# Attention followed by a spectral mix on one core: q and k transposed in one pass, one pair's x moved ahead of a chunk, idle products at two places

## The chip, the core and the metric

The kernel runs on one core of a Trainium2 chip. The metric is the device time of one execution in microseconds (us). The kernel before takes 443.85 us, the median of three runs (443.67 to 444.85). The profile was taken in a run of 444.44 us and spans 442.4 us; all times of single instructions below count from the start of that span.

A core has five engines with a queue each, and each works its queue strictly in order: TensorE (PE in the profile, with PEld for its weight loads), VectorE (DVE), ScalarE (ACT), GpSimd (POOL) and SyncE (SP). Transfers between memory and the core's SBUF run on 16 DMA engines; here GpSimd and SyncE issue them. TensorE writes its results to PSUM, from where VectorE or ScalarE copies them.

## What is computed

There are 8 batches of 8 heads with 576 tokens and head size 64. Causal attention with a bias from a running sum of `s` gives x with 512 features per token; then the tokens are mixed in the frequency domain with 64 complex modes, and a dense layer with relu follows.

```python
# attention, per batch and head
scores = q @ k.T / sqrt(64)
cum    = cumsum(max(s, 0))
scores = where(causal, -1e9, scores + min(-(cum[:, None] - cum[None, :]), 0))
x      = softmax(scores) @ v                     # heads side by side: 512 features
# mix of the tokens
X = rfft(x, axis=tokens)[:64 modes]
Y = complex product of X with (w_r + i w_i)      # one 512x512 matrix per mode
u = x + irfft(Y)
out = u + max(u @ w_ch, 0)
```

The weights `w_r` and `w_i` are 64 matrices of 512x512 each, in float32 in memory, and are turned into bf16 by the transfer. They are most of what the kernel reads.

## The kernel before

**Attention.** The heads go in pairs: there are N = 32 steps n, each for one batch and two heads (n = 8 g + b, with g the group of 128 features and b the batch). A step works like this. `transposes(n + 1, half)` (lines 332 to 347) turns q and k of the next step around: the loaded tile holds q on partitions 0 to 63 and k on partitions 64 to 127 (two heads of 32 rows each), and every row holds 18 tokens one after the other. For nine tokens of a half, a 64x64 product transposes q into PSUM partitions 0 to 63 and another transposes k into partitions 64 to 127, 18 small products in all. Then two copies of 64x576 take q to the tile `qt` and k to the tile `kt`: in the first half both on VectorE, in the second half q on VectorE and k on ScalarE. The PSUM tile `tr_ps` has one buffer, so the second half's products follow the first half's copies. `scores` (line 366) multiplies keys and queries and takes the exponential on ScalarE (line 390), `av` (line 401) multiplies with v and divides by the sum on VectorE (lines 423 to 428), `fft` (line 435) takes the token transform of the step before, with four copies on VectorE (line 453).

The order of the work in a step is written out by hand (lines 564 to 592): scores of the first head, `av` of the step before, mode products if there are any, `transposes(n+1, 0)`, scores of the second head, `transposes(n+1, 1)`, `fft(n-1)`, `av(n, 0)`. In the last six steps (n = 26 to 31) x of six pairs of token tiles is transposed and multiplied with `w_ch` as well, in two parts of a step (`first_transposed`, `first_product`); the second part's product follows a copy on VectorE (line 538).

**The weights.** GpSimd issues all loads of q, k, v and the weights (line 234), in the order of their use. Weights come in tiles of four modes, 256 KB per transfer and two transfers per tile; a buffer is loaded again once its last product is done. `modes(g, c)` (line 455) multiplies chunk c (eight modes) of group g: 16 products, four for each of the chunk's four weight tiles.

**The end.** After attention the chunks of the last group (g = 3) come one by one (lines 833 to 856); between them lies work that doesn't need the weights: x of the remaining pairs is transposed (`x_transposed`, line 629) and multiplied with `w_ch` (`x_times_wch`, line 641), and y of each chunk is transposed (`y_transposed`), multiplied (`y_times_wch`) and spread (`gather`, `spread`). In the kernel before, x of pair 1 is transposed after the products of chunk 6, and multiplied with `w_ch` between y of chunk 6 and its product (lines 852 to 856). The products of chunk 7, the last, come in four lots of four, numbered 0 to 3 (line 471); lots 0 and 1 use the real weights, lots 2 and 3 the imaginary ones. Ahead of lot 2 stand ten products for the results of pair 0 (`first_u`, `first_z(0)`), ahead of lot 3 eight for pair 1 (`first_z(1)`), line 868. After lot 3 the last y is finished and the 18 pairs of output tiles follow in a list written out by hand (lines 924 to 930).

PSUM tiles with the tag `aux` share two buffers in turn, at the end for the products of a chunk (`yp`), the transposed y (`yt_ps`) and its product (`v_ps`).

Of the kernel before, what the change touches and what calls it, by code (L numbers as in the profile page):

```python
# [9 lines left out]
FP32 = mybir.dt.float32  # L10
FP16 = mybir.dt.float16
BF16 = mybir.dt.bfloat16
# [6 lines left out]
def kernel(  # L19
# [11 lines left out]
    nc = tc.nc  # L31
    B, H, S, D = q.shape
    NM = moe_w_r.shape[0]
    DM = H * D
    P = 128
# [4 lines left out]
    NG = DM // P  # L40
# [6 lines left out]
    NCK = NM // MC  # L47
# [4 lines left out]
    RP = P // 4  # L52
    R = S // RP
    RH = R // 2
    W = 2 * P
    NWN = S // W
    NK = 2 * NWN
    HM = NM // 2
    HP = P // 2
# [45 lines left out]
    ident16h = gp.tile([P, P], FP16, name="ident16h")  # L105
    Ff_sb = gp.tile([P, NT, 3 * NM], FP16, name="Ff_sb")
    G_sb = gp.tile([P, SP], FP16, name="G_sb")
    wch_sb = gp.tile([P, DT, DM], FP16, name="wch_sb")
# [12 lines left out]
    NQ = 2  # L121
# [165 lines left out]
    with tc.tile_pool(name="cum_psum", bufs=1, space=PSUM) as cpsum:  # L287
        spos = s_sb
        zer, cum = (p_sb[i][:NPAIR, :].bitcast(FP32)[:, :S] for i in (0, 1))
        nc.vector.memset(zer, 0.0)  # L290
        nc.vector.tensor_scalar(out=spos, in0=s_sb, scalar1=0.0, scalar2=None, op0=ALU.max)
        nc.vector.tensor_tensor_scan(
            out=cum, data0=spos, data1=zer, initial=0.0, op0=ALU.add, op1=ALU.add
        )
        nc.vector.tensor_scalar(out=ncum_sb, in0=cum, scalar1=-8.0, scalar2=None, op0=ALU.mult)
        ct_ps = cpsum.tile([P, NK + 1, NPAIR], FP32, name="ct_ps")
        keys = cum[:, : NF * P].rearrange("c (w p r) -> c w r p", p=P, r=2)
        for x in range(NK):
            nc.tensor.transpose(
                ct_ps[:, x, :], keys[:, x // 2, x % 2, :], ident32[:NPAIR, :NPAIR]  # L300
            )

        tl = p_sb[2][:NPAIR, :].bitcast(FP32)[:, : 2 * NL].rearrange("p (x t) -> p x t", x=2)
        for x in range(2):
            nc.vector.tensor_copy(out=tl[:, x, :], in_=cum[:, (NT - 1) * P :])
        nc.tensor.transpose(
            ct_ps[:, NK, :], tl.rearrange("p x t -> p (x t)"), ident32[:NPAIR, :NPAIR]
        )
        nc.vector.tensor_copy(out=cumt_sb, in_=ct_ps)
        for x in range(2):  # L310
            rows = slice(NL * x, NL * x + NL)
            nc.vector.tensor_copy(
                out=cumt4[rows, :], in_=cumt_sb[rows, NK, x::2]
            )
# [17 lines left out]
    def transposes(n, half):  # L332
        if n >= N:
            return
        src = loaded[n][:, n % 2, :].rearrange("p (r d) -> p r d", d=D)[:, half * RH : half * RH + RH]
        ps = trpool.tile([P, RH, 2 * RP], BF16, name="tr_ps", tag="tr")
        for r in range(RH):
            for i in range(2):
                rows = slice(HP * i, HP * i + HP)
                nc.tensor.transpose(ps[rows, r, :], src[rows, r, :], ident16[rows, rows])  # L340
        for i, dst in enumerate((qt, kt)):
            copy = (nc.vector.tensor_copy, nc.scalar.copy)[half * i]
            to = dst[n % NQ][:D].rearrange("d h (p r) -> d h p r", r=R)
            copy(  # L344
                out=to[:, :, :, half * RH : half * RH + RH],
                in_=ps[HP * i : HP * i + HP].rearrange("d r (h p) -> d h p r", h=2),
            )

    def scores4(n, ps):

# [293 lines left out]
    def x_times_wch(i, last):  # L644
        for x in range(2):
            start_z(i, x)
            for dt in range(DT):
                nc.tensor.matmul(  # L648
                    zs[i, x], xts[i][:, x, dt, :], wch_sb[:, dt, :],
                    start=(dt == 0), stop=(last and dt == DT - 1), skip_group_check=True,  # L650
                )
# [25 lines left out]
    def y_times_wch(c, yt):  # L677
        vp = auxpool.tile([P, DM], FP32, name="v_ps", tag="aux")
        for dt in range(DT):
            nc.tensor.matmul(  # L680
                vp, yt[:, dt, :], wch_sb[:, dt, :], start=(dt == 0), stop=(dt == DT - 1)
            )
        vb = spool.tile([P, DM], FP16, name="v_sb", tag="v")
        nc.vector.tensor_copy(out=vb, in_=vp)
        spread(c, 1, vb)
        return vb

    def gather(c0, c1, turns, kinds):

        n = 2 * MC * (c1 - c0)  # L690
        rows = slice(2 * MC * c0, 2 * MC * c1)
        ng = P // n
        for b0 in range(0, B, ng):
            for which in kinds:
                ps = auxpool.tile([P, DM], FP32, name="g_ps", tag="aux")
                for dt in range(DT):
                    for g in range(ng):
                        op = yt_first[:, dt, : c1 - c0].rearrange("p c (x b) -> p (c x) b", b=B)
                        nc.tensor.matmul(
                            ps[n * g : n * g + n, :] if which else ps[n * g : n * g + n, bass.ts(dt, P)],  # L700
                            op[:, :, b0 + g],
                            wch_sb[:, dt, :] if which else ident16h,
                            start=(dt == 0 or not which), stop=(dt == DT - 1 or not which),
                            tile_position=(0, n * g), skip_group_check=True,
                        )
                for g in range(ng):
                    dst, src = yv[rows, b0 + g, which, :], ps[n * g : n * g + n, :]
                    if g % 2:
                        nc.vector.tensor_copy(out=dst, in_=src)
                    else:  # L710
                        nc.scalar.copy(out=dst, in_=src)
            if b0 // ng in turns:
                work()
# [119 lines left out]
    for c in range(NCK - 2):  # L833
        yb = modes(NG - 1, c)
        for x in range(TAKE[c] - 1):
            work()
        if c == NCK - 3:
            x_transposed(0)
        yt = y_transposed(yb, c)
        if TAKE[c]:  # L840
            work()
        if c >= NY:
            if c == NCK - 3:
                x_times_wch(0, False)
            y_times_wch(c, yt)
            if c == NCK - 3:
                gather(NY, NCK - 2, (), (0,))
        elif c == NY - 1:
            gather(0, NY, (1, 3), (1, 0))
    assert not order_z and not ahead  # L850
    c = NCK - 2
    yb6 = modes(NG - 1, c)
    x_transposed(1)
    yt = y_transposed(yb6)
    x_times_wch(1, False)
    vb6 = y_times_wch(c, yt)


    def first_u():
        add_x(0)  # L860
        add_y(u_of(0), 0, 0, slice(0, GK))
        add_last(u_of(0), 0, yb6, c=0)

    def first_z(i):
        add_y(z_of(i), i, 1, slice(0, GK))
        add_last(z_of(i), i, vb6, c=0)

    yb = modes(NG - 1, NCK - 1, {2: lambda: (first_u(), first_z(0)), 3: lambda: first_z(1)})

    yt = spool.tile([P, DT, P], FP16, name="yt_sb", tag="yt")  # L870
    for x in range(2):
# [95 lines left out]
```

The softmax here doesn't subtract the row's maximum and nothing guards it: scores larger than these inputs give would overflow.

## Time and profile before

| | before |
|---|---|
| median of 3 runs | 443.85 us |
| profiled span | 442.4 us |
| TensorE busy, products | 340.4 us (77%), 4364 instructions |
| VectorE busy | 253.3 us (57%) |
| ScalarE busy | 226.2 us (51%) |
| bytes moved | 93.25 MB, mean 211 GB/s |
| attention, first q and k products to the end of its last step | 10.7 to about 336 us |
| first products of the last chunk of weights | 403.5 us |
| last transfer of weights issued | 397.2 us |
| first output transfer issued | 413.4 us |

The page has one row for each group of instructions: line, engine, operation, what it writes and reads, shape and count, then busy time and mean duration of one in ns, then the idle time of the engine ahead of them and what ended it. Its second part cuts the span into 40 slices of 11.06 us and gives busy tenths; PEclk is the granted TensorE clock in tenths. The chain of waits follows the work that ended last back to the start. The timeline gives merged rows in order of time: start, length, engine, line, operation, count, and in brackets the idle time ahead.

### The profile page before, as it was taken

The numbers are of one execution on the slowest core, as the hardware profiler recorded it, in microseconds if no ns is written. First come the engines' busy times: TensorE is split into PE (matmuls) and PEld (weight loads), VectorE is DVE, ScalarE is ACT, GpSimd is POOL, SyncE is SP. The second block draws the span as 40 slices with busy tenths as digits, with TensorE's granted clock in tenths as the row PEclk, the third lists the DMA queues.
The fourth block names the chain that finished last, engine by engine and source line by source line (L and its number), as shares of the span: only waits on it lengthen the run. The fifth ranks groups of instructions, "written<-read, shape, count | busy, mean of one in ns | idle before, by whom it ended". The sixth has DMA issues, their size and how long they took to land.

```text
span 442.4 us, 10783 instructions
## 1 busy us (share of the span) xinstructions
PE 340.4 (77%) x4364; PEld 208.2 (47%) x4411; DVE 253.3 (57%) x574; ACT 226.2 (51%) x421; POOL 246.1 (56%) x385
## 2 busy tenths in 40 slices
PE   1788988988776996593946918888887987759994
PEld 0455665655444653361634505555653445423441
DVE  7766776665645664462633605767655454442696
ACT  1476787365645643472543604665660534320794
POOL 7766565565565656455655546455544444440495
PEclk9998999998969798987895978999997999988998
DMA  9999999999999999999999999999999999997498
GB/s 180 202 208 204 204 206 205 206 207 206 208 195 206 205 208 205 209 206 209 203 206 206 208 207 198 207 206 206 202 209 211 209 209 210 210 217 150 147 388 344
DMA packets 72768, 93.25 MB, mean 211 GB/s; under 512 B 29760, under 2 KB 31296, under 8 KB 72720
## 3 DMA queue, kind: packets, MB, share of 16 engines
q0 software_dynamic: 63408, 81.29, 104.9%
q1 hardware_dynamic: 9312, 11.29, 7.6%
q8 instruction: 34, 0.56, 0.5%
q14 instruction: 14, 0.11, 0.1%
HBM read 163.51 MB, written 9.44 MB: 391 GB/s over the span
## 4 chain that ended last, share of the span: by engine, by line
DMA 60%; PE 19%; DVE 7%; POOL 6%; issue 4%; ACT 2%; POOLq 0%; DVEq 0%
DMA w_sb<-in_moe_w_i_dram 31%; DMA w_sb<-in_moe_w_r_dram 16%; DMA qk<-in_k_dram 8%; PE yp L463 4%; PE sc_ps L382 3%; DMA x_all<-in_moe_w_r_dram 2%; POOL w_sb L234 2%; DMA qk<-in_q_dram 2%; PE sc_ps L376 2%; DMA y_acc<-in_moe_w_r_dram 2%; PE z_ps L546 2%; DVE xt L538 2%; DVE xs L453 1%; PE z_ps L648 1%; PE av_ps L418 1%
## 5 line engine op out<-in xcount | busy, mean ns | idle before, releaser
L390 ACT ACTIVATE p_sb<-sc_ps,cumt_sb 128x576 f16<-128x576 f32 (+1 forms) x256 | 141.7, 635 | 34.3 <-PE sc_ps L382 33.9
L234 POOL DMA_DIRECT2D w_sb<-in_moe_w_r_dram x120 | 71.2, 595 | 63.2 <-DMA w_sb<-in_moe_w_i_dram 16.7
L234 POOL DMA_DIRECT2D w_sb<-in_moe_w_i_dram x120 | 70.9, 593 | 53.0 <-DMA w_sb<-in_moe_w_i_dram 18.7
L344 DVE COPY qt<-tr_ps 64x576 bf16<-64x576 bf16 x64 | 47.8, 747 | 55.7 <-PE tr_ps L340 55.6
L234 POOL DMA_DIRECT2D v<-in_v_dram x72 | 52.0, 722 | 36.6 <-DMA w_sb<-in_moe_w_r_dram 7.6
L382 PE MATMUL sc_ps<-qt,kt 128*128 128x320 bf16 (+2 forms) x337 | 66.7, 303 | 7.2 <-ACT kt L344 3.4
L340 PE MATMUL tr_ps<-ident,qk 64*64 64x64 bf16 x1152 | 35.4, 206 | 38.9 <-DMA qk<-in_k_dram 18.0
L463 PE MATMUL yp<-w_sb,xs 128*32 128x512 bf16 (+1 forms) x480 | 43.2, 413 | 23.8 <-DMA w_sb<-in_moe_w_i_dram 16.8
L361 ACT ACTIVATE p<-sc_ps,cumt 128x64 f16<-128x64 f32 x32 | 10.0, 313 | 88.7 <-PE sc_ps L357 88.7
L376 PE MATMUL sc_ps<-negm,ident 128*128 128x256 bf16 x256 | 53.8, 295 | 0.0
L382 PEld LDWEIGHTS <-kt 128*128 128x128 bf16 x384 | 39.0, 105 | 31.1 <-ACT kt L344 8.8
L340 PEld LDWEIGHTS <-qk 64*64 64x64 bf16 x1152 | 26.9, 119 | 55.2 <-DMA qk<-in_k_dram 19.0
L418 PE MATMUL av_ps<-v,p_sb 128*128 128x65 f16 x1024 | 43.8, 197 | 1.4 <-DVE x_all L428 1.0
L418 PEld LDWEIGHTS <-p_sb 128*128 128x128 f16 x1024 | 37.4, 99 | 8.5 <-DVE x_all L428 3.7
L453 DVE CAST xs<-ft_ps 64x128 bf16<-64x128 f32 x128 | 36.6, 286 | 3.7 <-PE ft_ps L443 2.2
L463 PEld LDWEIGHTS <-xs 128*32 128x32 bf16 (+1 forms) x512 | 19.3, 144 | 41.3 <-DMA w_sb<-in_moe_w_i_dram 15.0
L423 DVE TENSOR_REDUCE den<-av_ps 128x5 f32<-128x10 f32 x64 | 10.8, 169 | 41.4 <-PE av_ps L418 40.4
L428 DVE TENSOR_TENSOR x_all<-av_ps,rcp 128x320 f16<-128x320 f32 x64 | 31.5, 492 | 2.2
L344 ACT COPY kt<-tr_ps 64x576 bf16<-64x576 bf16 x32 | 22.9, 715 | 15.4 <-DVE qt L344 14.8
L443 PE MATMUL ft_ps<-Ff_sb,x_all 128*64 128x192 f16 (+1 forms) x320 | 25.2, 274 | 1.0 <-DVE x_all L428 1.0
L648 PE MATMUL z_ps<-wch_sb,xs 128*128 128x512 f16 x96 | 25.3, 412 | 0.2 <-DVE xs L639 0.2
L344 DVE COPY kt<-tr_ps 64x576 bf16<-64x576 bf16 x32 | 24.4, 762 | 0.4
(113 smaller groups left out, 423.9 us busy)
## 6 DMA issues: line engine op xcount, KB each, us to landing
w_sb<-in_moe_w_r_dram POOLq DMA_DIRECT2D x120, 256.0 KB, 8.4
w_sb<-in_moe_w_i_dram POOLq DMA_DIRECT2D x117, 256.0 KB, 9.0
out_dram<-r_w SPq DMA_DIRECT2D x16, 512.0 KB, 2.8
v<-in_v_dram POOLq DMA_DIRECT2D x72, 64.0 KB, 7.4
qk<-in_q_dram POOLq DMA_DIRECT2D x15, 288.0 KB, 8.3
qk<-in_k_dram POOLq DMA_DIRECT2D x15, 288.0 KB, 9.2
x_all<-in_moe_w_i_dram POOLq DMA_DIRECT2D x6, 256.0 KB, 8.0
y_acc<-in_moe_w_r_dram POOLq DMA_DIRECT2D x4, 256.0 KB, 7.0
```

The source lines that it names most:

```text
L234: nc.gpsimd.dma_start(out=dst, in_=src)
L340: nc.tensor.transpose(ps[rows, r, :], src[rows, r, :], ident16[rows, rows])
L344: copy(out=to[:, :, :, half * RH : half * RH + RH], in_=ps[HP * i : HP * i + HP].rearrange("d r (h p) -> d h p r", h=2),)
L376: nc.tensor.matmul(ps[:, bass.ds(w * S, W)], ident16, negm[:, bass.ts(r, W)], start=True, stop=False, skip_group_check=True,)
L382: nc.tensor.matmul(ps[:, c0 : c0 + i1 - i0], keys[:, w, r, :], qh[:, i0:i1], start=False, stop=True, skip_group_check=True,)
L390: nc.scalar.activation(out=pt[:, poff[x] : poff[x] + S - w * W], in_=ps[:, w * S : (w + 1) * S - w * W], func=ACTF.Exp, bias=cumt_sb[:, x, ...
L418: nc.tensor.matmul(ps[:, I, r : r + NCH], lhsT, rhs, start=(i == 0), stop=(i == len(todo) - 1), skip_group_check=True,)
L428: nc.vector.tensor_tensor(out=x_all[:, g, b, :, D * h : D * h + D], in0=ps[:, :, 1 : NCH], in1=rcp.unsqueeze(2).to_broadcast([P, NT, D]), ...
L443: nc.tensor.matmul(ps[HP * q_ : HP * q_ + HP].rearrange("p h f -> p (h f)"), x_all[:nT, g, b, T, q_::2], Ff_sb[:nT, T, :], start=(T == 0), ...
L453: nc.vector.tensor_copy(out=xs[g % 2][HP * h : HP * h + HP, q_, :, h, :, b, :], in_=a)
L463: nc.tensor.matmul(ps[32 * cg : 32 * cg + 32, :], cols[k0:, q_, 1 - ri, :, c * MC // 2 + cg], wt[(g, c, ri, cg // 2)][k0:, 2 * (cg % 2) + ...
L648: nc.tensor.matmul(zs[i, x], xts[i][:, x, dt, :], wch_sb[:, dt, :], start=(dt == 0), stop=(last and dt == DT - 1), skip_group_check=True,)
```

## The change

Three edits.

1. **Transposes.** One product now transposes q and k of one token together: all 128 rows of the loaded tile are taken, the result is 64 features on 64 partitions, with 128 columns (q of both heads, then k of both heads). Tokens go in twos: the even one of a two lands on PSUM partitions 0 to 63, the odd one on 64 to 127. A step has 18 products instead of 36. The halves of a step are five and four twos (`SPLIT`). The copies out of PSUM are four per half instead of two: 64x320 in the first half and 64x256 in the second. In the first half all four are on VectorE; in the second the order is q on VectorE, k on ScalarE, q on VectorE, k on ScalarE. They write every second token of `qt` and `kt`.
2. **x of pair 1.** `x_transposed(1)` moves from behind chunk 6 to chunk 5, right after the product of pair 0, and `x_times_wch(1)` to behind the last `gather`, still ahead of chunk 6.
3. **Idle products.** 46 products of 128x64 with the identity stand ahead of the first transposes of the running sum, and four of 128x512 ahead of lot 3 of the last chunk. Nobody reads their results. They are to keep TensorE busy at places where it waits. The second tile for them, `idle_ps`, takes a turn of the two `aux` buffers between `v_ps` of chunk 6 and `yp` of chunk 7.

```diff
+    SPLIT = (0, (RH + 1) // 2, RH)
...
+        idle_ps = cpsum.tile([P, HP], FP32, name="idle_ps")
+        for i in range(46):
+            nc.tensor.matmul(idle_ps, ident16, ident16[:, :HP], start=True, stop=True, skip_group_check=True)
         ct_ps = cpsum.tile([P, NK + 1, NPAIR], FP32, name="ct_ps")
...
-        src = loaded[n][:, n % 2, :].rearrange("p (r d) -> p r d", d=D)[:, half * RH : half * RH + RH]
-        ps = trpool.tile([P, RH, 2 * RP], BF16, name="tr_ps", tag="tr")
-        for r in range(RH):
-            for i in range(2):
-                rows = slice(HP * i, HP * i + HP)
-                nc.tensor.transpose(ps[rows, r, :], src[rows, r, :], ident16[rows, rows])
-        for i, dst in enumerate((qt, kt)):
-            copy = (nc.vector.tensor_copy, nc.scalar.copy)[half * i]
-            to = dst[n % NQ][:D].rearrange("d h (p r) -> d h p r", r=R)
-            copy(
-                out=to[:, :, :, half * RH : half * RH + RH],
-                in_=ps[HP * i : HP * i + HP].rearrange("d r (h p) -> d h p r", h=2),
-            )
+        r0, r1 = SPLIT[half : half + 2]
+        src = loaded[n][:, n % 2, :].rearrange("p (r y d) -> p r y d", y=2, d=D)
+        ps = trpool.tile([P, SPLIT[1], P], BF16, name="tr_ps", tag="tr")
+        for r in range(r0, r1):
+            for y in range(2):
+                nc.tensor.transpose(ps[HP * y : HP * y + HP, r - r0, :], src[:, r, y, :], ident16)
+        for y in range(2):
+            for i, dst in enumerate((qt, kt)):
+                copy = nc.scalar.copy if half and i else nc.vector.tensor_copy
+                to = dst[n % NQ][:D].rearrange("d h (p r y) -> d h p r y", r=RH, y=2)
+                copy(
+                    out=to[:, :, :, r0:r1, y],
+                    in_=ps[HP * y : HP * y + HP, : r1 - r0, HP * i : HP * i + HP].rearrange(
+                        "d r (h p) -> d h p r", h=2
+                    ),
+                )
...
             if c == NCK - 3:
                 x_times_wch(0, False)
+                x_transposed(1)
             y_times_wch(c, yt)
             if c == NCK - 3:
                 gather(NY, NCK - 2, (), (0,))
+                x_times_wch(1, False)
...
     yb6 = modes(NG - 1, c)
-    x_transposed(1)
     yt = y_transposed(yb6)
-    x_times_wch(1, False)
     vb6 = y_times_wch(c, yt)
...
-    yb = modes(NG - 1, NCK - 1, {2: lambda: (first_u(), first_z(0)), 3: lambda: first_z(1)})
+    idle_ps = auxpool.tile([P, DM], FP32, name="idle_ps", tag="aux")
+
+    def idle_products(n):
+
+        for i in range(n):
+            nc.tensor.matmul(idle_ps, ident16h, wch_sb[:, 0, :], start=True, stop=True, skip_group_check=True)
+
+    yb = modes(NG - 1, NCK - 1, {2: lambda: (first_u(), first_z(0)), 3: lambda: (first_z(1), idle_products(4))})
```

## The prediction

> **What bounds the kernel now.** I read the slices of the span first, then the chain of waits, then the timeline around three places. The slices (rows: granted TensorE clock, DMA share, rate):
>
> ```profile
> PEclk9998999998969798987895978999997999988998
> DMA  9999999999999999999999999999999999997498
> GB/s 180 202 208 204 204 206 205 206 207 206 208 195 206 205 208 205 209 206 209 203 206 206 208 207 198 207 206 206 202 209 211 209 209 210 210 217 150 147 388 344
> ```
>
> Up to slice 35 (398 us) the DMA engines are never idle and the rate is 195 to 217 GB/s, whatever the compute engines do. The stream of loads is a belt of fixed length; compute can lengthen it only by holding back an issue until the belt runs dry. The transfers issued at 394.70, 395.89 and 397.19 took 10.7, 10.3 and 10.2 us to land: 405.4, 406.2 and **407.4**. What follows is the end. The chain of waits there (start, length, what):
>
> ```profile
> 386.01 10.89 DMA w_sb<-in_moe_w_i_dram
> ...
> 396.95 1.07 PE yp L463 x4
> 398.02 0.96 PE xt_ps L635 x16
> 398.98 0.54 PE yt_ps L672 x4
> 399.52 3.18 PE z_ps L648 x8
> 402.70 0.86 PE v_ps L680 x4
> ...
> 406.43 0.58 PE yp L463 x4
> 407.01 0.55 PE z_ps L744 x4
> 407.56 0.43 PE z_ps L755 x4
> 408.00 0.60 PE yp L463 x4
> 408.62 0.44 DVE y_sb L487
> ```
>
> From 396.95 TensorE is the chain without a gap, and the eight products of pair 1 (L648) take 3.18 us because the clock was half (0.50 from 395.5 to 402 in a table of half microseconds). But lot 3 starts at 407.9 to 408.0 while its weights landed at 407.4: only 0.5 us of that long chain is more than the belt.
>
> Then, in the timeline, how the two readers of one transposed tile stand, and what queues behind them on VectorE in one of the last attention steps:
>
> ```profile
> 35.59 0.75 DVE L344 COPY qt<-tr_ps 64x576 bf16<-64x576 bf16 x1 [0.57 <-PE tr_ps L340]
> 36.37 0.71 ACT L344 COPY kt<-tr_ps 64x576 bf16<-64x576 bf16 x1 [1.08 <-DVE qt L344]
> ...
> 309.30 0.74 DVE L344 COPY qt<-tr_ps 64x576 bf16<-64x576 bf16 x1
> 309.96 1.18 DVE L453 CAST xs<-ft_ps 64x128 bf16<-64x128 f32 x4
> 310.23 0.71 ACT L344 COPY kt<-tr_ps 64x576 bf16<-64x576 bf16 x1
> 312.01 0.68 DVE L538 CAST xt<-xt_ps 128x512 f16<-128x512 f32 x1
> 312.74 1.04 PE L546 MATMUL z_ps<-wch_sb,xt 128*128 128x512 f16 x4 [1.00 <-DVE xt L538]
> ...
> 86.02 0.73 POOL L234 DMA_DIRECT2D v<-in_v_dram  x1 [2.81 <-PE av_ps L418]
> 379.86 2.37 POOL L234 DMA_DIRECT2D w_sb<-in_moe_w_r_dram  x4 [3.28 <-PE g_ps L699]
> ```
>
> ScalarE, idle, starts its copy 0.03 us after VectorE's ended: the readers take turns. From 275.9 to 339.5 the chain is compute alone (TensorE, then VectorE's copies, then the product of L546). The last two lines are clear places where GpSimd was held back by TensorE and not by landings.
>
> **What the Trainium skill says.** (1) "PSUM — Partial Sum Buffer", section on bank collisions: two engines must not touch one bank and quadrant of partitions at once, reads included, so software keeps them apart. The trace agrees and is stricter: q and k lie in different partitions of `tr_ps`, and still no copy on ScalarE starts before VectorE's has ended. (2) "TensorE: Matmul & The Clock Gate", "What's actually happening": the clock is half or full and follows activity in windows of about 3.4 us. The trace agrees: eight such products take 1.90 us at 387.8 and 3.18 us in the chain above. (3) "TensorEngine Tiling (Array Packing)", "Instruction Overhead": a small product costs about 60 cycles whatever its size. The trace shows 18 in a row of 0.47 us, less than that: products on different parts of the array overlap.
>
> **Transposes, part by part.** TensorE: 36 products with 64 columns become 18 with 128, in twos on separate column halves. Before, the first 17 of a half fit into 0.47 - 0.19 = 0.28 us, 16 ns each, as if twos overlapped. If twos still overlap: 5 x 53 = 0.27 and 4 x 53 = 0.21 us; if not, 0.53 and 0.43. I take -0.1 us a step (bounds -0.15 and +0.4). Copies: VectorE's 576 columns take 747 to 762 ns; its rows of 128 and 512 columns (286 and 686 ns) give 1.04 ns a column and 153 ns fixed, so 486 ns for 320 columns and 419 for 256. A step on VectorE: 2 x 747 + 762 = 2256 ns before, 4 x 486 + 2 x 419 = 2782 after, **+0.53 us**. ScalarE: 715 ns becomes two of 715 - 320 x 0.83 = 450 ns ("ScalarE: Activation LUTs", "What ACT_TABLE_LOAD costs", has 0.833 ns an element; the trace's exponentials at 320 and 576 columns, 530 and 740 ns, give 0.82). Writing every second element isn't in the trace; at least nothing, at most double time. I take nothing.
>
> The second half is now q, k, q, k on two engines in turn: a new wait. VectorE's second q stands behind ScalarE's first k, which stands behind the exponentials (L390, ended at 310.20 here). So it starts about 310.23 + 0.45 = 310.7, and the four xs copies behind it at 311.15, where they started at 309.96: about +1.0 us with what the first half adds (+0.4 - 0.1). The product of L546 and everything behind it on TensorE moves with them. In the chain 275.9 to 339.5 that is **+1.0 us in each of five steps**, 5 us. Earlier steps run 6.6 us apart (q copies at 41.19, 47.81, 54.43): there kt is ready +0.7 us later.
>
> What of this reaches the end? TensorE waits 1.88 us for weights at 355.71 and 2.06 at 396.95; chunk 6's wait and the four us taken out behind it absorb the rest of the five. The belt feels it only where GpSimd is held. At 86.02 the delay is 6 steps x 0.7, less 1.18 us waited for k at 68.13, less about 1 us for a warmer start, plus 1.4 for two more steps: some 3 us. The last transfer in flight then (issued at 82.61, 8.1 us) lands at 90.8, so the belt thins but hardly empties: +0.5 us (0 to 1.5). At 379.86 TensorE would be 5 - 2 = 3 us late, and transfers in flight last to 385.7: +0.3 us (0 to 1). **Sum +0.8 us** (0 to 2.5).
>
> **x of pair 1.** Its 16 small products (0.5 us) and 8 large ones (1.8 us) go ahead of chunk 6. TensorE idles 1.9 us ahead of 393.71 for the yv copies and 2.06 ahead of 396.95 for weights; they fit, and VectorE's two copies (1.28 us) push the v copy of chunk 5 back 0.6 us at most, hidden by the same weights. This takes 4 us out of the chain behind 396.95.
>
> **Idle products and the end.** At the start 46 products run at 53 ns cold (64 columns at half clock), 2.5 us from 6.6 us on, done before the scan that the next products await (9.7): no cost, perhaps a full clock before 19.8. At the end: chunk 6 done 397.6, y 398.3, transposed and copied 399.3, v_ps to 400.2 (401.1 cold). `idle_ps` turns the two buffers, so chunk 7's first product now waits for the copy of v_ps (0.69): 401.0; hidden, since lot 1's weights land at 391.95 + 10.0 = 402.0. Then 0.5 and ten products of 0.215: 404.7; lot 2's weights land at 405.4; lot 2 and its eight products 0.58 + 0.98; four idle products 4 x 0.215 = 0.86: lot 3 at **407.9**, where it was. The idle products eat the 0.5 us. Gain 0.1 us; best -0.5 (lot 3 at 407.4). If the thin stretch 395.5 to 401 halves the clock until 405.5, the ten products take up to 4.3 us: +1.0.
>
> Behind lot 3 nothing changes; 34 us follow as before. About 1,100 fewer instructions of 10,783, at 0.56 MB of fetches (queue 8), spare 0.06 MB of 207 GB/s: -0.2 us.
>
> Sum: 443.85 + 0.8 - 0.1 - 0.2 = **444.3 us**.
>
> **Rivals.**
> - *The turns starve the belt* (30%). The delay at 86 us is the full 6 us and at 380 us 4 or 5, each dries the belt for about 1.5 us, and the end runs cold once (+0.5): 443.85 + 3.0 + 0.5 - 0.3 = 447.0. For: VectorE and ScalarE already alternate; VectorE is busy 4.5 of the 5 us from 30 to 35. Against: TensorE's transposes wait 30 us for q and k in all, so many steps have slack.
> - *Compute comes early* (20%), faster: the warm start and cheaper transposes let GpSimd issue without the holds at 86 and 380, which thin the belt by perhaps 1 us together, and lot 3 starts at 407.4: 443.85 - 1.0 - 0.5 - 0.2 = 442.1. Against: the rate shows no dip at 86 (204 GB/s in 85 to 90).
> - *Forecast, no change* (50%): 444.3.
>
> **Numbers.** Range 441.8 to 447.4: it reaches 0.3 to 0.4 us past each rival's time, and leaves out about a third of each rival's cases, 0.17 in all. Within 0.3% is 442.5 to 445.2: nine in ten of the forecast's cases, and few of the rivals'. Faster 0.20, same 0.45, slower 0.35.
>
> **What would show it.** Six copies on VectorE near 486 and 419 ns (others would mean that the spaced writes cost); ScalarE's first k ahead of VectorE's second q in all 32 steps; the hold at 86 us longer by 2 to 4 us; the step distance of 6.6 us near 7.3; the last landing at 407 to 409; lot 3 starting where the idle products end. A last landing before 406.5, or VectorE's copies without turns, would prove me wrong.

## The result and the profile after

The changed kernel takes **469.22 us**, the median of six runs (464.58 to 471.41), against 444.2 for the kernel before (443.43 to 444.92). The ratio is 1.0548, 95% interval 1.049 to 1.0607: **slower by 5.5%**, where I had forecast 444.3 and a range up to 447.4. The profile is of the shortest of the six runs, span 462.8 us, 20.4 more than before. Medians and ratios in this document count the runs within 1.5% of the fastest of their kernel, which leaves out two of the four of one experiment, tr_qqkk (458.43 and 459.37 us).

The slices of the changed kernel, one digit or rate for each 11.57 us of the span:

```profile
DMA  9999999959999999999999999999989999995398
GB/s 179 196 184 206 203 205 206 205 98 170 207 204 207 205 208 205 209 206 208 204 207 206 208 206 207 206 208 202 206 131 171 191 210 208 209 214 108 115 384 342
```

The belt of loads, full from end to end before, has two holes: counted from 0, slices 8 and 9 (93 to 116 us) and 29 to 31 (335 to 370 us). The same in stretches of 10 us (start and end, then length, busy time of each engine with its count, granted clock, DMA share, GB/s):

```profile
90.00:100.00 10.00, 5.79 (x89) 3.65 (x87) 7.51 (x20) 5.53 (x11) 2.10 (x4) 0.99 0.96 163
100.00:110.00 10.00, 9.90 (x120) 5.42 (x121) 5.39 (x11) 2.57 (x6) 5.82 (x10) 0.84 0.50 82
...
340.00:350.00 10.00, 6.46 (x91) 3.94 (x88) 8.53 (x19) 5.61 (x11) 4.74 (x8) 1.00 0.84 130
350.00:360.00 10.00, 9.03 (x102) 5.65 (x104) 4.80 (x13) 5.79 (x11) 4.75 (x8) 1.00 0.93 159
```

The kernel before has 207, 205, 210 and 210 GB/s in these four. With 193 and 197 GB/s in the stretches at 330 and 360 (before: 210 and 209), the lost rate is (44 + 123) x 10 / 205 = 8.1 us in the first hole and (17 + 80 + 51 + 12) x 10 / 210 = 7.6 us in the second, 15.7 us of belt. The last weights are issued at 411.66 instead of 397.19, 14.5 us later.

What made the first hole is one row of GpSimd's timeline (start, length, line, what it loads, and in brackets the idle time ahead). First the kernel before, the first products with weights from the buffers that are loaded again, and the transfer into one of them; then the same in the changed kernel:

```profile
82.12 1.96 PE L463 MATMUL yp<-w_sb,xs 128*32 128x512 bf16 x32
91.28 0.59 POOL L234 DMA_DIRECT2D w_sb<-in_moe_w_r_dram  x1 [0.84 <-PE av_ps L418]
```

```profile
91.52 0.62 POOL L235 DMA_DIRECT2D w_sb<-in_moe_w_r_dram  x1
102.84 2.49 PE L470 MATMUL yp<-w_sb,xs 128*32 128x512 bf16 x32
104.16 0.59 POOL L235 DMA_DIRECT2D w_sb<-in_moe_w_r_dram  x1 [12.02 <-PE yp L470]
```

GpSimd is held 12 us because TensorE hasn't used the weights in the buffer it is to fill; transfers in flight run out meanwhile. Before, the buffer was free some 8 us ahead of GpSimd. The second hole is of the same kind: from 322.7 to 373.2 us GpSimd waits five times for such products, 4.42, 8.83, 7.88, 6.15 and 3.81 us. Over the whole run its waits for them were 2.9 us before, the longest 1.9, and are 50.1 now, the longest 12.0 (us in total, times, longest):

```profile
POOL w_sb L234 <- PE yp L463: 2.9, 2, 1.9
POOL w_sb L235 <- PE yp L470: 50.1, 9, 12.0
```

And why TensorE is late is seen on VectorE. First one step of the kernel before, then one of the changed kernel, both from the middle of the first group:

```profile
47.81 0.74 DVE L344 COPY qt<-tr_ps 64x576 bf16<-64x576 bf16 x1
48.56 0.76 DVE L344 COPY kt<-tr_ps 64x576 bf16<-64x576 bf16 x1
49.89 0.75 DVE L344 COPY qt<-tr_ps 64x576 bf16<-64x576 bf16 x1 [0.57 <-PE tr_ps L340]
50.57 1.18 DVE L453 CAST xs<-ft_ps 64x128 bf16<-64x128 f32 x4
...
53.60 0.17 DVE L423 TENSOR_REDUCE den<-av_ps 128x5 f32<-128x10 f32 x1 [0.90 <-PE av_ps L418]
...
54.43 0.74 DVE L344 COPY qt<-tr_ps 64x576 bf16<-64x576 bf16 x1
```

```profile
56.36 0.71 DVE L349 COPY qt<-tr_ps 64x320 bf16<-64x320 bf16 x1
56.92 0.72 DVE L349 COPY kt<-tr_ps 64x320 bf16<-64x320 bf16 x1
57.66 0.72 DVE L349 COPY qt<-tr_ps 64x320 bf16<-64x320 bf16 x1
58.23 0.71 DVE L349 COPY kt<-tr_ps 64x320 bf16<-64x320 bf16 x1
59.45 0.66 DVE L349 COPY qt<-tr_ps 64x256 bf16<-64x256 bf16 x1 [0.51 <-PE tr_ps L344]
60.83 0.65 DVE L349 COPY qt<-tr_ps 64x256 bf16<-64x256 bf16 x1 [0.72 <-ACT kt L349]
61.51 1.19 DVE L460 CAST xs<-ft_ps 64x128 bf16<-64x128 f32 x4
...
64.55 0.17 DVE L430 TENSOR_REDUCE den<-av_ps 128x5 f32<-128x10 f32 x1 [0.90 <-PE av_ps L425]
...
65.39 0.71 DVE L349 COPY qt<-tr_ps 64x320 bf16<-64x320 bf16 x1
```

From first copy to first copy a step takes 54.43 - 47.81 = 6.62 us before and 65.39 - 56.36 = 9.03 after. The two waits in brackets of before are short, and the transposes that the first is for wait themselves for VectorE's copies out of the one PSUM tile (first before, then after):

```profile
PE tr_ps L340 <- DVE kt L344: 8.5, 16, 1.9
PE tr_ps L344 <- DVE kt L349: 44.2, 32, 2.9
```

So I read this row of work as a closed loop that sets the distance of the steps; the runs with added copies below test that. The first half went from 2.08 us (47.81 to 49.89) to 3.09, the second (up to the xs copies) from 0.68 to 2.06, the rest from 3.86 to 3.88. So +1.01 and +1.38, together the 2.4 us. The copies themselves (mean ns after the busy time):

```profile
L349 DVE COPY qt<-tr_ps 64x320 bf16<-64x320 bf16 x64 | 45.8, 716 | 0.5
L349 DVE COPY kt<-tr_ps 64x320 bf16<-64x320 bf16 x64 | 45.6, 713 | 0.0
L349 DVE COPY qt<-tr_ps 64x256 bf16<-64x256 bf16 x64 | 41.7, 651 | 37.0 <-ACT kt L349 22.9 <-PE tr_ps L344 14.0
L349 ACT COPY kt<-tr_ps 64x256 bf16<-64x256 bf16 x64 | 41.6, 650 | 60.3 <-DVE qt L349 60.3
```

I had 486, 419 and 450 ns. The end adds the remaining 20.4 - 14.5 = 5.9 us: lot 3 starts 16.55 us behind the last issue (428.21), where it was 10.73 us before. There the weights are no longer the limit: the last transfer took 11.1 us and landed at 422.8. The chain is TensorE and the copies it waits for on VectorE and ScalarE, with TensorE's clock at 0.50 from 421 to 424 us. In TensorE's timeline, pair 1's eight products, which the change moved forward, now run right ahead of chunk 6, whose products run as one row of 16 without a wait for weights, and the idle products stand right ahead of lot 3:

```profile
414.50 1.90 PE L655 MATMUL z_ps<-wch_sb,xs 128*128 128x512 f16 x8
416.44 1.09 PE L470 MATMUL yp<-w_sb,xs 128*32 128x512 bf16 x16
...
427.25 1.04 PE L880 MATMUL idle_ps<-wch_sb,ident16h 128*128 128x512 f16 x4
428.21 0.65 PE L470 MATMUL yp<-w_sb,xs 128*32 128x512 bf16 x4
```

### The profile page after: what moved, and what is told of

Read it like the earlier page. It is cut to its first block, busy times and chain, and to the rows that moved or that the text cites. A ratio compares the mean times of both kernels' runs of the same rounds, so it can differ in the third digit from the quotient of the medians.

```text
span 462.8 us, 9886 instructions
## 1 busy us (share of the span) xinstructions
PE 343.1 (74%) x3847; PEld 202.6 (44%) x3885; DVE 305.8 (66%) x670; ACT 245.4 (53%) x453; POOL 246.3 (53%) x385
## 4 chain that ended last, share of the span: by engine, by line
DVE 34%; PE 29%; DMA 22%; ACT 6%; issue 4%; POOL 3%; POOLq 0%; SPq 0%; DVEq 0%; ACTq 0%
DVE qt L349 12%; DMA w_sb<-in_moe_w_i_dram 10%; DMA w_sb<-in_moe_w_r_dram 9%; PE yp L470 6%; DVE xs L460 5%; DVE kt L349 5%; PE z_ps L655 4%; PE av_ps L425 4%; DVE x_all L435 3%; ACT kt L349 3%; PE sc_ps L389 2%; PE tr_ps L344 2%; DMA qk<-in_k_dram 2%; POOL w_sb L235 2%; PE z_ps L553 2%
## 5 line engine op out<-in xcount | busy, mean ns | idle before, releaser
L349 DVE COPY qt<-tr_ps 64x256 bf16<-64x256 bf16 (+1 forms) x128 | 87.5, 683 | 37.5 <-ACT kt L349 22.9
L389 PE MATMUL sc_ps<-qt,kt 128*128 128x320 bf16 (+2 forms) x346 | 71.6, 315 | 17.2 <-DVE qt L349 13.6
L349 ACT COPY kt<-tr_ps 64x256 bf16<-64x256 bf16 x64 | 41.6, 650 | 60.3 <-DVE qt L349 60.3
L344 PE MATMUL tr_ps<-ident,qk 128*64 128x128 bf16 x576 | 29.6, 232 | 44.2 <-DVE kt L349 44.2
L425 PE MATMUL av_ps<-v,p_sb 128*128 128x65 f16 x1024 | 46.8, 202 | 13.1 <-DVE x_all L435 12.2
L425 PEld LDWEIGHTS <-p_sb 128*128 128x128 f16 x1024 | 39.7, 103 | 23.1 <-DVE x_all L435 19.3
L349 DVE COPY kt<-tr_ps 64x320 bf16<-64x320 bf16 x64 | 45.6, 713 | 0.0
L344 PEld LDWEIGHTS <-qk 128*64 128x64 bf16 x576 | 18.9, 113 | 58.4 <-DVE kt L349 51.2
L383 PEld LDWEIGHTS <-ident 128*128 128x128 bf16 x256 | 19.1, 104 | 11.8 <-issue 3.4
L450 PE MATMUL ft_ps<-Ff_sb,x_all 128*64 128x192 f16 (+1 forms) x320 | 22.4, 251 | 1.0 <-DVE x_all L435 1.0
```

The source lines that it names most:

```text
L344: nc.tensor.transpose(ps[HP * y : HP * y + HP, r - r0, :], src[:, r, y, :], ident16)
L349: copy(out=to[:, :, :, r0:r1, y], in_=ps[HP * y : HP * y + HP, : r1 - r0, HP * i : HP * i + HP].rearrange("d r (h p) -> d h p r", h=2),)
L383: nc.tensor.matmul(ps[:, bass.ds(w * S, W)], ident16, negm[:, bass.ts(r, W)], start=True, stop=False, skip_group_check=True,)
L389: nc.tensor.matmul(ps[:, c0 : c0 + i1 - i0], keys[:, w, r, :], qh[:, i0:i1], start=False, stop=True, skip_group_check=True,)
L425: nc.tensor.matmul(ps[:, I, r : r + NCH], lhsT, rhs, start=(i == 0), stop=(i == len(todo) - 1), skip_group_check=True,)
L450: nc.tensor.matmul(ps[HP * q_ : HP * q_ + HP].rearrange("p h f -> p (h f)"), x_all[:nT, g, b, T, q_::2], Ff_sb[:nT, T, :], start=(T == 0), ...
```

## The experiments

**Theory:** the copies, dearer than costed and in turns, lengthen each step; TensorE comes late to the mode products, GpSimd is held, the belt runs dry. **Rivals:** the moved x of pair 1 and the idle products cost by themselves; the wider products cost; or only one of the two causes on the copies' side is real (their length, or their turns).

### Which edit it is

The copy edit alone, and everything but the copy edit.

```diff
 # tr_only: the changed kernel without
-    idle products (start and end)
-    x_transposed(1), x_times_wch(1, False) at chunk 5 (back behind chunk 6)
 # no_tr: the changed kernel with transposes() of the kernel before
```

> The kernel before with the transposes and copies of the changed kernel alone; x of pair 1 and the idle products as before. Theory (the new copies lengthen every attention step, TensorE comes late, GpSimd is held back and the stream of loads runs dry): nearly all of the 25 us stay, 465 to 472 us, copies near 650 and 715 ns. Rival (the moved x of pair 1 and the idle products cost at the end, since in the changed kernel they stand on TensorE between weights that have landed and their products): 4 us or more less, 458 to 465 us.

> The changed kernel with the transposes and copies of before: the move of x of pair 1 and the idle products alone. Theory: 443.7 to 444.5 us against 444.2, since lot 3 of the last chunk waits for weights that land at 407.4 us as before. Rival (these two edits cost by themselves): 446 to 449 us. If the warm clock at the start and at the end helps, 442.5 to 443.5 us.

tr_only took 472.11 us (ratio 1.0621, 1.0595 to 1.0647), no_tr 446.19 (1.004, 1.0026 to 1.0055). The copy edit is the whole of the loss. The other two edits cost 0.4% beside the old copies, just inside the rival's 446 to 449 and far from 25 us; what it is comes below. Beside the new copies they seem to give 3 us back (472.1 against 469.2), but the two intervals overlap.

### Which part of the copy edit

Tokens r and r + 9 share a two, so each copy writes runs of neighbours:

```diff
-        src = loaded[n][:, n % 2, :].rearrange("p (r y d) -> p r y d", y=2, d=D)
+        src = loaded[n][:, n % 2, :].rearrange("p (y r d) -> p r y d", y=2, d=D)
...
-                to = dst[n % NQ][:D].rearrange("d h (p r y) -> d h p r y", r=RH, y=2)
+                to = dst[n % NQ][:D].rearrange("d h (p y r) -> d h p y r", r=RH, y=2)
...
-                    out=to[:, :, :, r0:r1, y],
+                    out=to[:, :, :, y, r0:r1],
```

> The changed kernel with tokens r and r+9 put together instead of 2r and 2r+1: the same products, the same copies in the same order on the same engines, but each copy writes runs of five (or four) neighbouring tokens where the changed kernel writes every second one. Theory A (writing two-byte elements at a stride of two is what makes a copy dear): copies fall to about 490 and 420 ns, steps to about 7.5 us apart, 446 to 456 us. Theory B (the shortness of the inner loop, five or four elements, or the stride of the PSUM read, is dear): copies stay within 30 ns of 716 and 651, time 465 to 472 us.

450.54 us (1.0143, 1.0115 to 1.0172), 18.7 us less than the changed kernel. Theory A. The groups of this run:

```profile
L349 DVE COPY qt<-tr_ps 64x320 bf16<-64x320 bf16 x64 | 33.4, 521 | 12.8 <-PE tr_ps L344 12.4
L349 DVE COPY qt<-tr_ps 64x256 bf16<-64x256 bf16 x64 | 32.0, 500 | 38.2 <-ACT kt L349 21.4 <-PE tr_ps L344 16.7
```

The shorter copy did not fall to 420, though, and its mean hides two kinds, seen on VectorE's timeline (the first writes tokens 5 to 8 of each 18, the second 14 to 17):

```profile
54.01 0.57 DVE L349 COPY qt<-tr_ps 64x256 bf16<-64x256 bf16 x1 [0.51 <-PE tr_ps L344]
55.23 0.43 DVE L349 COPY qt<-tr_ps 64x256 bf16<-64x256 bf16 x1 [0.65 <-ACT kt L349]
```

A run of four that starts at an odd token leaves two elements without their neighbour of the same four bytes; one that starts at an even token leaves none.

Next the order of the second half, with the spaced writes kept:

```diff
-        for y in range(2):
-            for i, dst in enumerate((qt, kt)):
+        for j in range(4):
+            y, i = (j % 2, j // 2) if half else (j // 2, j % 2)
+            for dst in ((qt, kt)[i],):
```

> The changed kernel with the second half's copies in the order q, q, k, k: both q on VectorE one after the other, then both k on ScalarE. VectorE no longer waits for ScalarE between its two copies. Theory (the length of the copies themselves sets the step): VectorE's wait for ScalarE (22.9 us in 32 steps) goes, but both k come behind both q, so 1 to 6 us are gained: 463 to 468 us. Rival (turns between the two engines are the main cost): 452 to 460 us.

453.4 us, from runs of 450.59 and 456.23 (1.0201, 1.0147 to 1.0256). VectorE's wait for ScalarE is gone, steps stand about 8.6 us apart, and the time lies in the rival's bracket: this order is worth some 16 us beside the spaced writes, and 10 even by the longest run, not 1 to 6. Neither mend alone brings the time back, and what they give alone (18.7 and some 16 us) is more than the whole loss of 25, so the two can't be added. Both together:

> The changed kernel with both mends: tokens r and r+9 put together, so that copies write runs of neighbours, and the second half's copies in the order q, q, k, k. Theory (VectorE's part of a step sets the distance of the steps; neighbours take 1.1 us off it, the order 0.7): the second q copies of a step stand 9.05 - 1.1 - 0.7 = 7.2 us apart in the first group, against 6.6 in the kernel before, and the holds of the loads nearly vanish: 444 to 448 us. Rival (what is left of the loss after either mend alone, 6 and 9 us, comes from elsewhere, the four copies as such or the end): 448 to 452 us.

**444.56 us** (1.0001, 0.9989 to 1.0014), steps 7.3 us apart. Nothing of the loss is left, with the wider products, eight copies a step and the other two edits in place. So the wider products cost nothing that shows. The two causes are the writes and the turns; the 0.7 us by which a step is still longer is hidden behind the belt.

Conversely, the kernel before with its copies cut in two and its second half in turns, nothing else:

```diff
+        for j in range(4):
+            i, (s0, s1) = j % 2, ((0, 5), (5, RH))[j // 2]
...
-                out=to[:, :, :, half * RH : half * RH + RH],
+                out=to[:, :, :, half * RH + s0 : half * RH + s1],
...
```

> The kernel before, its transposes as they were, with each copy of 64x576 cut in two (five tokens and four, runs of neighbours as before), in the order q, k, q, k in both halves: the number of copies and the turns of the changed kernel, without its transposes, its spaced writes and its other edits. Theory (turns and more copies lengthen the step, apart from any spacing): copies near 510 and 430 to 570 ns, steps about 7.8 to 8.0 us apart, 447 to 453 us. Rival (it is the new transposes or the spaced writes alone): steps near 6.8 us, 443.5 to 445.5 us.

450.93 us (1.0131, 1.0103 to 1.0159), steps 8.13 us apart, its copies 0.42 to 0.58 us by where their runs begin. More copies in turns cost 6.5 us without any of the change's other parts.

### What the writes cost

The copies' loops turned around, so that they read neighbours and write 36 bytes apart:

```diff
-                to = dst[n % NQ][:D].rearrange("d h (p r y) -> d h p r y", r=RH, y=2)
+                to = dst[n % NQ][:D].rearrange("d h (p r y) -> d h r p y", r=RH, y=2)
...
-                    out=to[:, :, :, r0:r1, y],
+                    out=to[:, :, r0:r1, :, y],
...
-                        "d r (h p) -> d h p r", h=2
+                        "d r (h p) -> d h r p", h=2
```

> The changed kernel with the loops of the copies turned around: the 32 rows innermost, so that a copy reads 32 neighbouring elements of PSUM and writes them 36 bytes apart. Theory A (an element of two bytes that is written alone, not beside its neighbour, costs about one more ns): 700 to 730 ns for 64x320 and 640 to 660 for 64x256, as in the changed kernel, 465 to 472 us. Theory B (inner loops of five and four elements, or the strided read, are dear): about 490 and 420 ns, 446 to 455 us.

648.85 us, one run. Both expectations fell:

```profile
L349 DVE COPY qt<-tr_ps 64x256 bf16<-64x256 bf16 x64 | 80.2, 1253 | 61.6 <-ACT kt L349 42.1 <-PE tr_ps L344 19.5
L349 ACT COPY kt<-tr_ps 64x256 bf16<-64x256 bf16 x64 | 80.1, 1251 | 198.0 <-DVE qt L349 198.0
```

The same 256 columns now take twice what they took at a stride of four bytes, and the same on both engines. Short inner loops are not the cost (they are 32 long here), but "alone in its four bytes" is not the whole of it either: how far apart the writes lie seems to count too. The reads changed their order with the writes, and no run separates the two here.

Then runs that all begin at an even token and have an even number of tokens, in the order q, q, k, k, without the idle products at the end:

```diff
+    PART = (((0, 6), (10, 4)), ((6, 4), (14, 4)))
...
+        for j in range(6):
+            for y, (r0, nr) in enumerate(PART[half]):
+                if j < nr:
+                    nc.tensor.transpose(ps[HP * y : HP * y + HP, j, :], src[:, r0 + j, :], ident16)
...
+                    out=to[:, :, :, r0 : r0 + nr],
```

> The changed kernel with the order q, q, k, k, with tokens put together so that every run of a copy begins at an even token and has an even number of them (0 to 5 with 10 to 13, then 6 to 9 with 14 to 17), and without the idle products ahead of lot 3. Theory (an element of two bytes without its neighbour of the same four bytes costs about one ns more): copies of 64x256 near 420 ns, of 64x384 near 550, steps about 7.0 us apart, 443.4 to 444.4 us against 444.4, since the stream of loads sets the time. Rival (the run's length sets the cost): 64x256 near 500 ns as with runs from odd tokens, steps 7.3, 444 to 445 us.

443.97 us (0.9995, 0.9983 to 1.0008): no difference from before that can be measured. The theory had 64x256 at 420 ns, the rival at 500. The groups:

```profile
L351 DVE COPY qt<-tr_ps 64x256 bf16<-64x256 bf16 x96 | 40.5, 422 | 22.2 <-PE tr_ps L344 21.4
L351 ACT COPY kt<-tr_ps 64x256 bf16<-64x256 bf16 x64 | 23.9, 373 | 22.5 <-DVE qt L351 21.0 <-PE ft_ps L452 0.6
L351 DVE COPY qt<-tr_ps 64x384 bf16<-64x384 bf16 x32 | 17.4, 542 | 27.4 <-PE tr_ps L344 27.3
```

So 64x256 costs 422 ns in whole pairs, 570 with half its elements alone, 651 with all alone at a stride of two elements, 1253 at a stride of 18. My formula from the rows of before (153 ns and 1.04 ns a column) gives 419 and 552: right for whole pairs, as for the runs of nine tokens of the kernel before (752 against 747), and too low where many elements stand alone. A price for one lone element doesn't come out: 128 of 256 add 148 ns, all 256 add 229, and one in nine in the kernel before adds nothing that shows.

### Is it only the distance of the steps

The kernel before with VectorE's first copy of each step made two, three and four times over (the line of delay3; delay1 has 1 and delay2 has 2 in place of the 3):

```diff
-        for i, dst in enumerate((qt, kt)):
+        for i, dst in ((0, qt),) * (1 + 3 * (half == 0)) + ((1, kt),):
```

> The kernel before with VectorE's first copy of a step made twice (one more of 747 ns, same data): the step is lengthened, and nothing else. Theory (VectorE's copies lie in the loop that sets the step, and steps up to about 7.3 us cost nothing since the loads set the time): steps 6.6 + 0.75 = 7.4 us apart, 444 to 446 us. Rival (a step's length shows at once): 32 x 0.75 = 24 us, or the part before the last group, 8 x 0.75 = 6 us: 450 us or more.

> The kernel before with VectorE's first copy of a step made four times (three more of 747 ns, same data). Theory (the distance of the steps alone makes the time of the changed kernel): steps 6.6 + 2.25 = 8.9 us apart against 9.0 in the changed kernel, 465 to 472 us, with the same dips of the rate near 95 to 110 and 330 to 360 us. Rival (what costs is the wider products of the transposes, or the turns of the two engines by something other than the length they add): 450 to 460 us.

> The kernel before with VectorE's first copy of a step made three times (two more, same data). The steps will stand 8.2 us apart if only the copies count, 9.3 if the wait that appeared with three more copies (10.15 us, 1.2 more than the copies) grows as they do. Theory (the time depends on the distance of the steps alone, whatever made it): at 8.2 us 451 to 457 us, at 9.3 us 472 to 480 us, on the line through the other kernels (7.9: 450.5, 9.0: 469 to 472, 10.15: 493.5). Rival (the wider products or the turns cost beside the distance): 5 us or more below that line.

delay1 took 444.62 us (1.0009, 0.9996 to 1.0022), delay2 461.96 (1.0382, 1.0346 to 1.0418), delay3 493.54 (1.1105, 1.1083 to 1.1126). The last overshot because its steps stood 10.1 us apart and not 8.9; VectorE's wait for the product with v had grown:

```profile
60.29 0.17 DVE L423 TENSOR_REDUCE den<-av_ps 128x5 f32<-128x10 f32 x1 [2.06 <-PE av_ps L418]
```

It was 0.90 us before; delay3's TensorE had an average clock of 0.83 there, 1.00 before. delay2 shows both kinds of step in one trace: between 41 and 94 us the steps with a clock of 0.99 or 1.00 last 8.20 or 8.21 us, those with 0.82 or 0.83 last 9.28 to 9.34. So a step at the lower clock is a microsecond longer; that TensorE's idle time in the longer steps lowers the clock is my reading and not tried by itself.

All kernels by the mean distance of five steps, from about 50 us on (starts of the xs copies; for the kernel before three steps), against the time (the trace of tr_qqkk is of the run of 459.37 us):

| kernel | step, us | median, us | ratio |
|---|---|---|---|
| before | 6.62 | 444.2 | 1 |
| aligned | 7.06 | 443.97 | 0.9995 |
| runs_qqkk | 7.31 | 444.56 | 1.0001 |
| delay1 | 7.42 | 444.62 | 1.0009 |
| tr_runs | 7.94 | 450.54 | 1.0143 |
| split | 8.13 | 450.93 | 1.0131 |
| tr_qqkk | 8.63 | 453.4 | 1.0201 |
| delay2 | 8.86 | 461.96 | 1.0382 |
| tr_only | 9.16 | 472.11 | 1.0621 |
| after | 9.18 | 469.22 | 1.0548 |
| delay3 | 10.1 | 493.54 | 1.1105 |
| tr_pinner | 14.8 | 648.85 | one run |

Up to 7.4 us a longer step costs nothing, from 7.9 on it costs. Where this limit comes from is seen at the transfer that was held 12 us. The products that free its buffer start at 82.12 us before, 89.05 in delay1, 92.84 in tr_runs, 95.24 in split and 99.39 in delay2, and GpSimd's wait there is 0.84, 0.85, 4.54, 6.81 and 10.61 us. Before, they start some 9 us ahead of the transfer, and the buffer is free about 8 us ahead; eight steps lie before them, so I estimate the slack at 1 us a step: 7.6 us.

The three kernels with pure delay have neither turns nor wider products. Straight lines from delay1 to delay2 and on to delay3 give 450.9 us at the step of tr_runs, 453.2 at that of split, 459.2 at tr_qqkk, 469.6 at tr_only and 470.1 at the changed kernel; measured are 450.5, 450.9, 453.4, 472.1 and 469.2. None lies more than about 2.5 us above the delays, so the distance makes nearly all of the loss, whatever lengthened it. I had set another mark ahead: delay2 5 us or more below the line through the other kernels would speak for a cost beside the distance. It lies 4.9 us below the line from tr_runs to tr_only, at that mark, but tr_qqkk, with wider products and spaced writes, lies 9 below (3 by its longest run), so I take it for the bend of the curve. With runs of one kernel up to 7 us apart, a few microseconds beside the distance are not excluded. delay2's slices have the first hole too (94 and 187 GB/s in slices 8 and 9), the second only faintly.

### The two other edits

> The kernel before with x of pair 1 moved, and nothing else. Theory: lot 3 of the last chunk starts when its weights have landed instead of behind the long chain, 0.4 to 0.6 us earlier, 443.4 to 444.2 us against 444.4. Rival (the move itself costs, by the copies that stand ahead of chunk 6's or by a colder clock behind it): 445 to 447 us, as with the move and the idle products together (446.2).

```diff
+                x_transposed(1)          # at chunk 5, as in the change
...
+                x_times_wch(1, False)
...
-    x_transposed(1)
...
-    x_times_wch(1, False)
```

444.44 us (0.9999, 0.9989 to 1.001), a little above the theory. Lot 3 starts at 407.97, before at 407.92. The moved work did leave the chain, but TensorE's clock was 0.50 from 400 to 405 us, the ten products ahead of lot 2 took 3.2 us instead of 2.3, and lot 3 follows them without a wait for weights. The last weights came no earlier either: they landed at 407.7, before at 407.4. Then the move with the idle products at the start only:

> The kernel before with x of pair 1 moved and with the 46 idle products at the start, but without the four ahead of lot 3. Theory (the four idle products eat what the move gave, and 0.3 us more): 444.0 to 444.6 us, as with the move alone (444.4). Rival (the idle products at the start cost, by instructions to fetch or by the heads' first steps): 445.5 to 446.5 us, as with all of them (446.2).

445.74 us (1.0028, 1.0019 to 1.0037). The rival: 46 products in a stretch in which TensorE is idle cost 1.3 us. In this trace the median output transfer took 4.1 us to land instead of 2.8, with the same bytes. Which of place and number it is:

```diff
-                nc.tensor.matmul(
+                for _ in range(1 + (w == r == 0 and (h == 0 or n < 14))):
+                    nc.tensor.matmul(
```

> The kernel before with x of pair 1 moved, no idle products, and 46 products of the attention steps made twice (the mask's first product, in every first head and in the second heads of steps 0 to 13): as many instructions on TensorE as with the 46 idle products, at another place. Theory (46 more products move the fetch of TensorE's last 16 KB of instructions into the output stream, where it delays one DMA engine): the fetch lies about 17 us ahead of the end, 445.4 to 446.0 us. Rival (the idle products cost where they stand, at the start): 444.0 to 444.7 us, as with the move alone.

445.89 us (1.0027, 1.0016 to 1.0039): the number, not the place. Nearly all of it is lost behind lot 3, which starts at 408.21 here and 408.08 in no_tr_noend, with spans of 443.9 and 443.8 us against 442.4 in x1_only. The DMA view of this run between 426 and 429 us, in the middle of the output:

```profile
q1 hardware_dynamic: 583, 1.13, 97.2%
q8 instruction: 1, 0.02, 2.7%
...
out_dram<-r_w SPq DMA_DIRECT2D x2, 512.0 KB, 4.3
```

One fetch of instructions among 583 output packets, and outputs that land in 4.3 us. In x1_only the fetch lies between 409 and 412 us, ahead of the output:

```profile
q1 hardware_dynamic: 144, 0.13, 15.2%
q8 instruction: 1, 0.02, 2.3%
```

That the number of instructions costs is shown; that it is by this fetch is the reading of where the traces differ, not tried by itself. It fits that runs_qqkk, with all 50 idle products but 827 instructions fewer than before, has its last fetch between 412 and 415 us, outputs that land in 2.9 us, and no loss.

## Why the prediction was wrong

- **Right:** the belt bounds the kernel, a longer step is felt through holds of GpSimd (14.5 of the 20.4 us in the profile), the new wait of VectorE for ScalarE is there in all 32 steps, and moving x of pair 1 gains nothing that shows (0.1 us forecast for it and the idle products, 0.0 measured for the move). Steps of 7.3 us would have cost nothing: runs_qqkk and delay1 stand there, at 444.6, and I had forecast 444.3 for that distance.
- **The step that failed:** "Writing every second element isn't in the trace; at least nothing, at most double time. I take nothing." It costs 716 - 486 = 230 ns on each of four copies, 651 - 419 = 232 on each of two, and 200 on ScalarE's. The upper bound I wrote down, double time, held it; I put neither it nor a middle value into the step distance or the range. tr_runs, where most of it is gone, puts it at 1.2 us a step (9.18 against 7.94) and 18.7 of the 25 us. The prediction named spaced writes as what other copy times would mean, but gave them no time in its sum. The Trainium skill has a price that I hadn't drawn on: "Vector Engine (DVE) Microarchitecture Reference", section 5.2, "Measured stream behaviour on trn2", gives 1.054 ns a column with all streams contiguous and 1.71 for a destination that hops 4 KiB at every element, for elements of four bytes and another operation. Taken as an estimate for these of two, that is 4 x 320 x 0.656 + 2 x 256 x 0.656 = 1,176 ns a step on VectorE; the runs have 4 x 230 + 2 x 232 = 1,384. They agree in kind and are dearer: 229 / 256 = 0.9 ns more an element at a stride of two, (1253 - 422) / 256 = 3.2 ns at a stride of 18.
- **The second term mis-sized:** "Earlier steps run 6.6 us apart (...): there kt is ready +0.7 us later." I counted the turns fully in the last five steps only. VectorE's second q, and the xs copies behind it, come late in every step, because VectorE's row is a loop that TensorE's waits hang on. With copies of nearly the costed size (tr_runs) the halves grew by 0.30 and 1.00 us: steps of 7.94, not 7.3, and 450.5 us, outside my range already.
- **The holds:** I read the waits ahead of 86.02 and 379.86 us as GpSimd held back by TensorE, since the view names TensorE there. They are not, as far as the runs show: the same two transfers wait 2.82 and 3.34 us in the changed kernel, and 2.65 to 3.06 and 3.26 to 3.67 in all others with steps up to 9.2 us, however late TensorE is. What ends them stays open. The hold of 12.0 us stands seven transfers further on, where GpSimd waited 0.84 before. The forecast was "the belt thins but hardly empties: +0.5 us" for the first and +0.3 for the second; the two holes cost 8.1 and 7.6 us of belt. With steps 2.4 us longer instead of 0.7, TensorE comes to its first mode products at 98.88 us instead of 79.10.
- **The end:** forecast as bound by weights. That held while the steps were short; in the changed kernel the end is bound by TensorE and the copies it waits for, and is 5.9 us longer.
- **Idle products at the start, "no cost":** 1.3 us beside the old copies, by their number, and nothing in runs_qqkk. The -0.2 us for about 1,100 fewer instructions (897 in the profile) can't be seen.
- **The rival** of starving turns had the direction and the mechanism, and 447.0 us for it; it too took the copies at their costed length.

## What to carry to other kernels

Before dividing copies, find out whether they lie in the loop that sets the distance of the steps: waits of half a microsecond on the engine for work that waits for it in turn are the sign, however idle the engine is on average. A kernel bound by its loads hides longer steps up to a limit and then charges a growing part of them: here 18 us for each us of step from tr_runs to tr_only, 25 from delay2 to delay3, 33 on to the one run of tr_pinner, with 32 steps. So ask how far the step is from that limit, which is how long the first buffer to be loaded again lies free before its transfer, and give an unknown cost its middle, not its least, value. A wait that the view puts down to an engine is worth comparing with a run in which that engine is later. Have copies of two-byte elements write runs of neighbours, best in whole pairs aligned to four bytes, and let both copies of one engine follow each other where two engines read one tile in turns.

## What was not expected of the hardware

- One PSUM to SBUF copy of 64x256 bf16 takes 422, 570, 651 or 1253 ns on VectorE by the layout of its writes (for 1253 the order of the reads changed too), and 373, 650 or 1251 on ScalarE (whole pairs, all single at a stride of two, at a stride of 18).
- Readers of one transposed tile on two engines take turns in the order q, q, k, k as well (ScalarE waits 58.0 us for VectorE's q in tr_qqkk): the order only chooses who waits. Whether the program or the memory keeps them apart, no run here shows.
- Longer steps come with a lower granted clock of TensorE and so grow further: three copies of 0.75 us added 3.5 us to a step (clock 0.83 against 1.00), and in delay2 steps at full clock last 8.2 us, at 0.82 or 0.83 9.3 us.
- 46 more small products lengthened a kernel of 444 us by 1.2 to 1.3 us at either of two places; the trace shows an instruction fetch in the middle of the saturated output in both cases.
